# Loading two weight blocks ahead of the transposes, spreading by pairs of offsets, and a new order of steps

## The chip, the cores and the metric

The kernel runs on one core of a Trainium2 chip. The metric is the device time in microseconds of one execution, as the median of several runs. The profile is one further execution, recorded instruction by instruction; its span runs from the first instruction to the last. Engines: PE is TensorE's matmul side and PEld its weight loads, DVE is VectorE, ACT is ScalarE, POOL is GpSimd, SP is SyncE, which here only issues DMA.

## What is computed

Two independent halves whose results are put side by side. Half A is attention with 32 heads of 20 channels over 2048 positions, in which each position looks at 8 earlier ones, 2 apart. Half B is a state-space layer: a kernel K of length 2048 for each of 640 channels from 192 complex exponentials, and its causal convolution with u.

```python
# A: x [1, 2048, 640], wqkv [640, 1920], wo [640, 640]
q, k, v = split(x @ wqkv)                       # 32 heads of 20
idx = pos[:, None] - 2 * arange(8)[None, :]     # masked where negative
attn = softmax(einsum("bhsd,bhswd->bhsw", q, k[idx]) * 20**-0.5)
a = einsum("bhsw,bhswd->bhsd", attn, v[idx]).reshape(1, 2048, 640) @ wo

# B: u [1, 2048, 640]; A, B, C complex [640, 192]; dt = exp(log_dt)
P = exp((dt * A)[:, :, None] * bf16(arange(2048)))
K = einsum("dn,dnl,dn->dl", C, P, dt * B).real
y = irfft(rfft(u, 4096) * rfft(K, 4096))[:2048] + u * Dskip
out = concatenate([a, y], axis=-1)              # [1, 2048, 1280]
```

The positions of B are taken in bf16, so above 256 many positions share one rounded value. K is therefore computed at few distinct values only and then spread to all positions by matrices of zeros and ones.

## The kernel before, in words

**Steps and their order.** The program is written as 1772 small steps, each an instruction or a short run of them, collected by `st(...)` under the name of a stage. Nothing runs when a step is collected. `run` (L191) then calls the steps in the order of the list of numbers `ORDER` (L20), and each engine works through its own instructions in exactly that order. A step that waits holds all later ones of its engine. So `ORDER` is the schedule, written out by hand or by a program that is not part of the kernel.

**Start.** Six parameter arrays of half B are loaded ("nat", L297). A tiny store on SyncE (L326) waits for two of them and holds back what follows in SyncE's queue: four DMA transposes that load x with channels on the partitions ("xT", L330), 512 positions each. GpSimd looks at one element of the same parameters ("peek", L336), then loads the weights of q and k (L342), looks at one element of xT (L347), and then loads u (L353) and the weights of v (L342). Two small stores (L332, L333) put zeros ahead of k and v. TensorE turns the parameters (L381 to L390) and DVE and ACT make from them exponentials, sines and cosines (L448 to L466); those of chunks 1 to 4 go through memory ("Gdram", L469).

**Half A.** For k, q and v, 5 channel tiles and 4 position blocks, five 128x512 matmuls make a projection (L587), ACT casts it (L590), and SyncE stores it (L592). Later, for 4 blocks of positions, DVE forms products (L748), TensorE sums them (L753), ACT takes the exponential (L756), the weights are normalised (L773 to L789), DVE multiplies v by them (L804), TensorE sums (L809), ACT casts (L812), and a last matmul with wo (L823), a cast (L826) and a store end it.

**Half B.** The 640 channels go in 5 chunks. For each chunk DVE builds two tables, X (L188 to L190) and Y (L188 to L190, L544), TensorE contracts them (L561, 512 small matmuls a chunk) and the result is stored ("Kdram", L568). It comes back as K2 (L662), and stage "g" spreads it (L668 to L681): four steps of matmuls, one for each quarter of the 32 channels (`tq`); in each, for 8 offsets `j`, one or two 0/1 matrices and 4 groups of partitions, a matmul with 64 (or 32) columns (L677); after each step ACT copies the bank out (L681). `f1` (L633) transforms u and K (L641, L646), which takes one channel at a time, stage "x" does the second transform and the product (L696 to L703), "back" the inverse (L717, L723), and the last matmuls with HB (L886) go together with u times Dskip into the output.

Of the kernel before, what the change touches and what calls it, by code (L numbers as in the profile page):

```python
# [20 lines left out]
1 3 8 9 24 0 4 5 7 6 26 338 30 31 32 33 35 34 36 37 51 329 39 74 327 17 38 73 80 77 40 41 42 43 44 79 78 76 53 55 45 48 334 50 56 46 61 102 16 81 71  # L21
336 335 321 333 52 54 47 58 49 57 62 60 59 128 63 64 75 25 72 103 332 326 104 129 130 108 131 123 67 105 109 21 18 19 132 66 110 111 106 133 724 118
124 125 92 65 119 27 29 126 121 337 120 93 107 94 95 68 70 127 87 122 112 89 88 20 28 82 83 84 96 294 293 97 296 295 113 297 90 91 298 85 98 99 100 86
726 727 114 115 730 116 300 134 299 301 302 192 117 731 135 303 136 150 137 101 194 725 69 728 23 22 193 304 138 305 168 306 151 195 153 152 186 169
729 732 187 170 171 308 847 307 843 188 189 310 309 317 312 311 142 145 766 190 146 762 763 143 144 147 174 198 760 761 767 339 196 172 139 314 313 2
141 148 149 199 154 315 844 848 316 764 765 706 331 330 325 322 328 324 197 707 323 811 845 318 841 319 173 320 340 175 176 180 342 341 191 155 177
200 178 710 343 344 210 201 346 345 202 708 812 712 768 709 711 846 849 182 181 204 713 805 806 836 348 347 211 837 213 212 183 214 184 850 842 856
349 809 810 156 205 179 807 808 834 206 162 207 835 832 833 714 203 350 838 839 157 215 185 351 352 721 719 158 159 717 163 722 164 165 245 247 851
857 353 852 854 813 140 160 371 370 354 208 209 161 246 239 275 718 720 715 840 413 716 408 355 403 356 357 166 375 374 376 377 378 379 380 381 383
382 384 385 386 387 388 389 410 219 778 784 358 167 359 11 372 373 391 390 398 393 392 240 218 407 414 409 723 779 416 855 853 417 785 222 782 226 224  # L30
241 242 257 248 360 780 783 395 394 249 781 276 361 746 362 363 742 277 278 397 396 402 364 243 223 399 786 279 744 743 401 747 217 400 365 366 367
420 423 424 426 419 745 425 427 428 220 411 415 406 405 251 412 250 404 748 749 750 735 221 736 259 737 739 455 738 258 260 740 430 429 791 792 281
261 431 432 733 368 734 252 454 253 418 789 790 787 254 255 434 433 458 459 788 793 741 435 794 461 460 269 462 463 244 436 465 464 795 437 421 422
216 280 751 752 13 466 467 225 753 754 757 758 771 772 282 271 283 755 756 775 262 227 256 10 469 468 284 270 287 776 769 770 456 470 471 482 229 285
457 472 473 272 288 273 474 228 230 475 233 476 477 231 438 478 479 369 773 774 759 439 1343 802 289 777 440 798 290 291 480 441 442 803 481 263 496
799 234 814 483 815 800 443 274 286 1342 796 235 801 236 797 237 264 265 485 266 444 484 267 1344 292 820 445 804 821 823 446 827 825 824 1345 447 232
1346 448 488 1347 268 495 490 487 493 491 1348 238 541 1350 828 497 449 1349 1352 498 829 1351 450 826 1353 830 831 492 451 504 1355 503 501 1356 1357
500 489 1354 494 486 499 1358 1359 816 502 1360 818 817 1361 1363 507 508 510 509 512 511 506 539 819 822 1362 538 1364 505 1365 1366 1367 1368 858
514 513 515 516 542 517 518 519 864 543 1369 545 544 452 1374 12 520 546 547 522 865 873 1370 863 875 867 549 548 862 1402 1371 521 550 551 866 1373
881 882 876 874 879 880 868 871 872 869 583 859 877 878 870 883 884 887 1387 888 889 890 885 540 886 901 895 1372 553 860 552 902 1375 555 554 1377  # L40
557 556 566 559 558 893 1376 894 896 903 905 904 1378 1401 906 897 898 899 900 891 892 523 14 1403 1379 1388 923 924 580 1389 561 919 917 920 921 453
918 922 926 560 943 944 1404 925 1405 941 939 940 937 907 942 938 945 563 911 562 912 1390 1391 908 909 910 564 565 946 524 525 15 1406 927 913 1381
1407 526 914 1380 916 1382 928 579 571 576 584 1392 527 933 934 960 929 931 1384 1383 932 930 978 567 936 1393 528 1385 1429 568 969 970 1395 1394
1396 1398 1428 935 569 973 974 975 961 962 861 965 1430 1397 529 530 531 532 574 966 581 1432 1431 1399 1400 1441 1386 585 1433 572 575 582 573 533
1486 578 976 1442 1434 963 977 1435 1436 534 1437 535 588 587 586 570 1438 1439 536 1443 1444 577 971 1440 1466 1445 1446 1447 1449 983 972 592 591
594 964 623 967 590 968 593 984 915 595 596 1413 985 1448 1450 1414 995 622 997 1451 1452 1453 986 597 598 1454 996 599 600 1455 601 602 626 627 628
629 603 631 630 998 1001 979 980 999 604 589 1415 1002 632 633 1416 1000 981 982 989 987 990 988 1417 1408 991 992 993 1410 994 605 1017 1037 1487
1411 1409 1018 635 634 625 1456 1457 1038 636 637 1056 1412 956 958 957 947 949 948 953 954 955 1033 1034 1035 1013 1490 1014 1420 1039 1019 1036 1040
1015 950 1016 1020 1021 661 1022 638 951 606 1514 1513 1517 1042 1418 1419 1009 639 537 1488 1423 664 641 1041 1007 1005 640 657 1006 952 607 1010
1003 608 666 1421 609 610 1425 1023 1424 624 1489 1491 1008 1004 1024 1465 1469 1467 611 1011 642 643 1029 1030 650 1027 1472 1492 645 644 1028 1012  # L50
646 647 1057 1063 1025 1468 1470 1473 1026 1058 1074 658 1474 663 655 1064 612 649 648 667 1476 656 662 613 1422 1471 614 1426 1059 1073 1060 1067
1068 1061 1069 1070 1079 615 1475 616 1477 1062 1479 1478 1071 1072 1480 1458 1459 1460 1065 1066 1462 1461 1481 617 1463 1464 1515 651 1483 1081 1032
1031 1482 618 619 1080 1093 1094 1091 1092 1516 1518 674 1484 652 653 659 1519 1427 620 672 1082 676 675 1521 1485 665 1097 1098 1077 1075 1076 1078
677 678 1520 1523 1089 668 671 679 680 654 681 682 684 683 685 660 669 670 687 673 959 1085 1090 1086 1505 1095 1096 1503 688 686 689 1504 1522 1083
1087 1084 1524 1088 1525 1052 1099 1053 1100 1054 1506 1498 1049 1050 1051 1043 1044 1101 1045 1102 1500 1105 1103 1046 1104 1106 1108 1129 1131 1048
621 1047 690 1130 1132 1507 1495 1135 1133 1136 1134 1119 1125 1107 1170 1120 1126 1551 1499 1138 1137 1123 1124 1109 691 1152 692 1121 1111 693 1110
1122 1112 1526 1527 1528 1115 1116 1113 1163 1572 1114 1153 1529 1159 1164 1530 1501 1531 1161 694 1154 1532 1155 1533 1160 1167 1169 1534 1535 695
1162 1156 1550 1536 1537 696 1117 1496 1168 1599 1502 1538 1539 1571 1165 1493 1157 1158 1166 1540 1541 1171 1172 1179 1180 1542 1494 1552 1177 1173
1175 1176 1174 1178 1510 1508 1553 1511 1509 1128 1554 1555 1556 1575 1573 1189 1185 1183 1190 1186 1598 1600 1118 697 1574 1181 1187 1191 1184 1192
1576 1544 1543 1545 1547 698 1193 1188 1194 1182 1546 1195 699 700 1548 1565 1564 1566 1197 1199 1577 1567 1127 1568 701 1569 702 1207 1497 1196 1558  # L60
1557 1561 1559 1055 1200 1198 1208 1602 703 1601 1549 1560 1604 1603 704 1562 1570 1209 1605 1563 1210 1512 1142 1606 1143 1607 1148 1201 1144 1149
1150 1608 1588 1211 1202 1205 1609 1212 1139 1206 1611 1145 1613 1204 1203 1610 1140 1589 1215 1590 1213 1580 1141 1214 1146 1147 1591 1216 1221 1231
1225 1222 1219 1578 1229 1612 1232 1226 1220 1227 1230 1228 1234 1217 1218 1247 1248 1249 1254 1255 1628 1252 1253 1250 1251 1581 1650 1256 1257 1579
1258 1262 1260 1263 1649 1683 1614 1688 705 1689 1691 1692 1693 1259 1265 1264 1272 1615 1261 1273 1223 1616 1268 1270 1269 1271 1286 1266 1267 1288
1287 1278 1289 1279 1617 1618 1619 1620 1621 1629 1151 1592 1224 1282 1595 1596 1283 1284 1280 1622 1281 1285 1593 1274 1275 1690 1698 1276 1277 1699
1582 1233 1594 1583 1730 1733 1734 1735 1290 1736 1291 1737 1738 1294 1295 1731 1732 1623 1624 1625 1626 1687 1302 1303 1694 1627 1306 1304 1292 1307
# [147 lines left out]
def kernel(  # L214
# [126 lines left out]
    def ld_w(i):  # L341
        PQ.dma_start(out=wqkv[i]()[:], in_=wsrc[:, :, D * i:D * i + D])  # L342

    for i in (1, 0):
        st(lambda i=i: ld_w(i))
# [591 lines left out]
```

The softmax here doesn't subtract the row's maximum and nothing guards it: scores larger than these inputs give would overflow.

## Time and profile before

| | before |
|---|---|
| time, median of 3 (lowest to highest) | 377.85 us (376.5 to 384.24) |
| span of the profiled run | 378.9 us |
| instructions | 14759 |
| granted TensorE clock, mean | 0.891 |
| DMA | 72.54 MB, mean 191 GB/s |
| ACT table loads | 13 of 1283 ns |

In the page, the busy time of an engine is the sum of its instructions with overlaps counted once. A group line reads: line, engine, operation, output from inputs, shape, count, then busy time and mean time of one, then the idle time of the engine just before these instructions and what ended it. In the list of waits, the engine and line that waited stand first, then what ended the wait, the total, the number of times and the longest. "Issue" means that the engine waited for nothing that the profile shows.

### The profile page before, as it was taken

To read this page: it belongs to the slowest core of one execution; us is meant where nothing else is said; L and a number is where in the kernel's file an instruction comes from. 1 tells how busy PE (TensorE), PEld (TensorE's weight loads), DVE (VectorE), ACT (ScalarE), POOL (GpSimd) and SP (SyncE) were. 2 spreads that over 40 slices of the span, in tenths; PEclk is the share of its full clock that TensorE was granted. 3 is DMA by queue.
4 is the path that set the end of the run, shared out by engine and by line. 5 is a ranking of instruction groups with operands and counts; after the bars stand their busy time and mean duration, and the time that the engine had idled before them with its cause. 6 is when DMAs were issued, how large, how long until landed. Compare 5 with 4: busy or idle time off the path is not lost.

```text
span 378.9 us, 14759 instructions
## 1 busy us (share of the span) xinstructions
PE 295.5 (78%) x6431; PEld 195.2 (52%) x6431; DVE 311.5 (82%) x467; ACT 274.1 (72%) x604; POOL 64.9 (17%) x123
## 2 busy tenths in 40 slices
PE   1704765999999992658889789679997799798872
PEld 1601222455545550636655557556775558576751
DVE  1891799798999999996999986999967956769770
ACT  2980998899999972369557667577867559898651
POOL 3021012110000003512402022005001211001181
PEclk9955896999999998589668889988999969999997
DMA  7999658656567648955908573243626979869777
GB/s 175 143 162 291 153 162 295 207 194 234 184 215 245 200 147 253 270 129 169 216 13 210 144 210 89 74 143 114 180 79 188 301 255 293 260 201 331 203 154 174
DMA packets 59696, 72.54 MB, mean 191 GB/s; under 512 B 24344, under 2 KB 49544, under 8 KB 58864
## 3 DMA queue, kind: packets, MB, share of 16 engines
q1 hardware_dynamic: 53760, 54.91, 50.8%
q0 software_dynamic: 5296, 15.96, 16.6%
q8 instruction: 50, 0.82, 0.9%
q10 hardware_dynamic: 576, 0.74, 0.6%
q14 instruction: 14, 0.11, 0.1%
HBM read 43.98 MB, written 24.98 MB: 182 GB/s over the span
## 4 chain that ended last, share of the span: by engine, by line
PE 25%; ACT 13%; DVE 11%; issue 8%; DMA 2%; ACTq 0%; SPq 0%; DVEq 0%
PE ps_f L641 5%; ACT S L700 5%; PE ps_op L823 5%; PE ps_k L561 4%; DVE p L804 3%; PE ps_ia L717 3%; ACT Z L723 3%; ACT A L646 3%; PE ps_f L696 2%; PE ps_l L753 2%; PE ps_o L809 1%; DVE Yf L703 1%; PE ps_s L677 1%; DVE krtmp L188 1%; DVE prod L748 1%
## 5 line engine op out<-in xcount | busy, mean ns | idle before, releaser
L587 PE MATMUL ps_p<-xT,w 128*128 128x512 bf16 x300 | 75.6, 402 | 27.2 <-DMA xT<-in_A_x_dram 17.6
L561 PE MATMUL ps_k<-Ytab,Xtab 128*20 128x33 bf16 (+1 forms) x2560 | 53.2, 245 | 14.5 <-DVE Ytab L544 9.0
L587 PEld LDWEIGHTS <-w 128*128 128x128 bf16 x300 | 28.9, 102 | 66.8 <-issue 36.9
L646 ACT CAST A<-ps_f 128x512 bf16<-128x512 f32 x80 | 44.1, 620 | 25.2 <-PE ps_f L641 14.1
L561 PEld LDWEIGHTS <-Xtab 128*20 128x20 bf16 (+1 forms) x2560 | 45.5, 126 | 27.5 <-issue 24.1
L748 DVE TENSOR_TENSOR prod<-qb,kb 128x2048 bf16<-128x2048 bf16 x40 | 47.1, 1219 | 7.1 <-PE ps_l L753 7.0
L804 DVE TENSOR_TENSOR p<-vb,attn 128x2048 bf16<-128x2048 bf16 x40 | 47.6, 1218 | 6.2 <-PE ps_o L809 6.1
L700 ACT CAST S<-ps_f 128x512 bf16<-128x512 f32 x80 | 43.0, 613 | 8.4 <-PE ps_f L696 4.5
L590 ACT CAST st<-ps_p 128x512 bf16<-128x512 f32 x60 | 33.5, 580 | 16.9 <-PE ps_p L587 16.8
L797 POOL DMA_DIRECT2D vb<-vd x40 | 22.0, 556 | 96.3 <-DVE p L804 92.0
L703 DVE TENSOR_TENSOR Yf<-S 128x1024 bf16<-128x1024 bf16 x40 | 26.4, 686 | 7.9 <-ACT S L700 6.1
L696 PE MATMUL ps_f<-A,cT 128*64 128x128 bf16 x640 | 28.8, 228 | 1.9 <-ACT A L646 0.9
L823 PE MATMUL ps_op<-wo,oT 128*128 128x320 bf16 x160 | 29.2, 327 | 0.6 <-ACT ob L826 0.6
L696 PEld LDWEIGHTS <-cT 128*64 128x64 bf16 x640 | 21.0, 113 | 11.3 <-issue 9.4
L522 ACT ACTIVATE Stab<-ta 128x192 bf16<-128x192 f32 x80 | 24.4, 367 | 0.1
L809 PE MATMUL ps_o<-p,cG 128*32 128x512 bf16 x160 | 17.4, 445 | 8.5 <-DVE p L804 7.7
L723 ACT CAST Z<-ps_ia 128x512 bf16<-128x512 f32 x40 | 21.5, 607 | 3.3 <-PE ps_ia L717 3.2
L717 PE MATMUL ps_ia<-cEA,Yf 64*128 64x128 bf16 x640 | 21.8, 221 | 1.6 <-ACT ysb L891 0.7
L641 PE MATMUL ps_f<-cBD,U 128*64 128x128 bf16 x320 | 21.6, 293 | 0.0
L717 PEld LDWEIGHTS <-Yf 64*128 64x128 bf16 x640 | 19.0, 96 | 4.8 <-issue 3.5
L641 PEld LDWEIGHTS <-U 128*64 128x64 bf16 x320 | 19.4, 205 | 3.1 <-issue 2.2
L188 DVE TENSOR_TENSOR krtmp<-Xtab,Xg 128x1536 bf16<-128x1536 bf16 (+2 forms) x30 | 20.5, 682 | 0.3 <-DMA Xtab<-Gdram 0.3
(105 smaller groups left out, 515.8 us busy)
## 6 DMA issues: line engine op xcount, KB each, us to landing
vb<-vd SPq DMA_DIRECT2D x40, 128.5 KB, 5.3
vb<-vd POOLq DMA_DIRECT2D x40, 128.5 KB, 4.2
Gdram<-cs SPq DMA_DIRECT2D x22, 192.0 KB, 2.9
HB<-k_HB SPq DMA_DIRECT2D x8, 512.0 KB
Zdram<-Z SPq DMA_DIRECT2D x3, 1024.0 KB
zq<-Zdram SPq DMA_DIRECT2D x12, 256.0 KB, 5.1
kb<-kd SPq DMA_DIRECT2D x4, 657.5 KB
us<-in_B_u_dram POOLq DMA_DIRECT2D x2, 1280.0 KB, 7.5
```

Source lines behind the costliest of these rows:

```text
L561: MM(ps()[32 * g:32 * g + 20, i, :], lhsT=X[c]()[rows, part % 2, :, col + t0 + i], rhs=Y[c]()[rows, :, part % 2, col + t0 + i], start=(par ...
L587: MM(ps()[:], lhsT=w()[:, kt, 128 * ct:128 * ct + 128], rhs=xT()[:, kt, 512 * sc:512 * sc + 512], start=(kt == 0), stop=(kt == 4))
L590: st(lambda so=so, sc=sc, ps=ps: ACTE.copy(out=so()[:, sc], in_=ps()[:]))
L641: MM(ps()[64 * r:64 * r + 64, jj], lhsT=src(16 * dd + 4 * jq + jj), rhs=BD1()[:, r, :], start=(jj == 0), stop=True, skip_group_check=True, ...
L646: st(lambda o=o, ps=ps: ACTE.copy(out=A1[c]()[:, :, sig, o:o + 16].rearrange("p k (j g) -> p k j g", g=4), in_=ps()[:].rearrange("p j (k g ...
L696: MM(ps()[64 * dd:64 * dd + 64, kk, r], lhsT=T()[:, k, r, :], rhs=A1[c]()[:, k, :, 64 * dd:64 * dd + 64], start=(kk == 0 and r == 0), stop ...
L700: st(lambda h=h, ps=ps, Sp=Sp: ACTE.copy(out=Sp()[:, :, :, :, 2 * h:2 * h + 2, :].rearrange("p r s j k g -> p (r s) j k g"), in_=ps()[:].r ...
L717: MM(ps[dd]()[:, jj].rearrange("p l r -> p (l r)"), lhsT=Yf[c]()[d, q, 4 * jq + jj, :], rhs=EA()[d, q, :], start=(jj == 0 and q == 0), sto ...
L723: st(lambda o=o, ps=ps, dd=dd: ACTE.copy(out=zc()[:, :, :, o:o + 4].rearrange("p l r j -> p (l r) j"), in_=ps[dd]()[:].rearrange("p j l r ...
L748: st(lambda pr=pr, ct=ct, u2=u2: V.tensor_tensor(out=pr()[:], in0=q()[:, ct].unsqueeze(1).to_broadcast([128, 4, PB]), in1=windows(k()[:, c ...
L804: st(lambda p2=p2, u2=u2: V.tensor_tensor(out=p2()[:], in0=v()[:, :, 2 * u2:2 * u2 + PB], in1=attn[b]()[:, u2].unsqueeze(1).to_broadcast([ ...
L823: MM(ps()[:], lhsT=oT[b]()[:, t, 128 * x:128 * x + 128], rhs=wo_sb()[:, t, 320 * eh:320 * eh + 320], start=(t == 0), stop=(t == 4))
```

## The change

It has four parts. First, the weights of q and k are loaded by GpSimd right after the parameters, and SyncE's tiny stores, which hold back the transposes, now wait for these weights instead of a parameter array; the weights of v and u follow, as before, behind a look at xT. The aim is that weight loads and transposes no longer share the DMA engines. Second, the spread goes by pairs of offsets: a step takes two offsets `j` and all 32 channels, so a matmul has 256 (or 128) columns in place of 64 (or 32), there are a quarter as many, and ACT's copy of a step fills two offsets of every channel instead of all offsets of eight channels. Third, all steps come in a new order; in SyncE's queue the constants Gs and RB and the two halo stores now stand ahead of the transposes, two of which are ahead of the first store to Gdram and two behind it. Fourth, the identity and the peeked element lie in another pool of SBUF.

```diff
 ORDER = """
-1 3 8 9 24 0 4 5 7 6 26 338 30 31 32 33 35 34 36 37 51 329 39 74 327 17 38 73 80 77 40 41 42 43 44 79 78 76 53 55 45 48 334 50 56 46 61 102 16 81 71
...
+16 3 8 9 0 4 7 5 1 17 6 31 32 33 19 18 21 10 12 34 20 26 27 25 24 28 36 35 38 37 53 39 75 40 41 42 322 74 78 333 326 77 55 81 43 44 57 49 73 72 45 46
...
-    ident = const("cst", "ident", np.eye(128), [128, 128])
+    ident = const("prep", "ident", np.eye(128), [128, 128])
...
-    tiny = dpool.tile([1, 2, 2], bf16, name="tiny")
+    peek = tl("prep", [1, 2, 2], bf16, "peek")
+    st.stage("igb")
+    st(lambda: PQ.tensor_copy(out=peek()[:], in_=nat[4][0]()[0:1, :, 0, 0:2]))
+    st.stage("iw")
+    wsrc = A_wqkv.rearrange("(kt k) c -> k kt c", k=128)
+    wqkv = [tl("xw", [128, 5, D], bf16, f"w{i}") for i in range(3)]
...
+    for i in (1, 0):
+        st(lambda i=i: ld_w(i))
+    tiny = dpool.tile([2, 2], bf16, name="tiny")
     st.stage("iga")
-    st(lambda: SP.dma_start(out=tiny[:], in_=nat[4][0]()[0:1, :, 0, 0:2]))
+    for i in (1, 0):
+        st(lambda i=i: SP.dma_start(out=tiny[i:i + 1], in_=wqkv[i]()[0:1, 4, D - 2:D]))
     st.stage("ix")
     xT = tl("xw", [128, 5, S], bf16, "xT")
...
-    peek = tl("cst", [1, 2, 2], bf16, "peek")
-    st.stage("igb")
-    st(lambda: PQ.tensor_copy(out=peek()[:], in_=nat[4][0]()[0:1, :, 0, 0:2]))
-    st.stage("iw")
...
-    for i in (1, 0):
-        st(lambda i=i: ld_w(i))
...
-        for tq in range(4):
-            ts = slice(8 * tq, 8 * tq + 8)
-            ps = bank([128, 8, 8, 8], "ps_s", "b")
-
-            def go(ts=ts, ps=ps):
-                for j in range(8):
-                    for n_, (w, par) in enumerate(plan[j]):
+        for jp in range(4):
+            ps = bank([128, 2, 8, 32], "ps_s", "b")
+
+            def go(jp=jp, ps=ps):
+                for jj in range(2):
+                    for n_, (w, par) in enumerate(plan[2 * jp + jj]):
                         sel = slice(0, 8) if par is None else slice(par, 8, 2)
                         for g in range(4):
-                            MM(ps()[32 * g:32 * g + 32, j, sel], lhsT=SEL()[:, w, :], rhs=K2()[:, g, sel, ts], start=(j == 0 and n_ == 0), stop=True,
+                            MM(ps()[32 * g:32 * g + 32, jj, sel], lhsT=SEL()[:, w, :], rhs=K2()[:, g, sel], start=(jj == 0 and n_ == 0), stop=True,
                                tile_position=(0, 32 * g), skip_group_check=True)
 
             st(go)
-            st(lambda ts=ts, ps=ps: ACTE.copy(out=K()[:, ts].rearrange("p t (b j) -> p t b j", j=8), in_=ps()[:].rearrange("p j b t -> p t b j")))
+            st(lambda jp=jp, ps=ps: ACTE.copy(out=K()[:].rearrange("p t (b j) -> p t b j", j=8)[:, :, :, 2 * jp:2 * jp + 2], in_=ps()[:].rearrange("p j b t -> p t b j")))
         f1(c, lambda t: K()[:, t], 1)
```

## The prediction

> **What bounds the kernel now.** I read the page's first part and the table by stages first, since no engine fills the span.
>
> ```profile
> PE 295.5 (78%) x6431; PEld 195.2 (52%) x6431; DVE 311.5 (82%) x467; ACT 274.1 (72%) x604; POOL 64.9 (17%) x123
> ```
>
> ```profile
> 0.00:20.00 20.00, 8.89 (x120) 7.59 (x120) 10.27 (x23) 12.09 (x34) 3.04 (x10) 0.99 1.02 152
> 20.00:40.00 20.00, 6.64 (x15) 1.94 (x15) 10.40 (x36) 8.73 (x29) 3.71 (x4) 0.50 1.11 239
> 40.00:145.00 105.00, 92.94 (x1361) 46.70 (x1361) 98.97 (x172) 97.47 (x208) 8.60 (x15) 0.97 0.63 204
> ...
> 300.00:379.00 79.00, 63.29 (x1412) 47.02 (x1408) 50.76 (x57) 54.42 (x116) 15.94 (x28) 0.93 0.81 236
> ```
>
> Columns: stretch, length, busy PE, PEld, DVE, ACT, POOL, then granted clock, DMA share and GB/s. VectorE carries the most work (311.5 us) and is idle for 67 us of the 378.9. From 40 to 145 us DVE, ACT and PE are all nearly full, so little is to be had there. The idle time lies at the start (10 us before the first data, 10 more between 20 and 40 us) and after 300 us (28 us, of which some 9 are the last projection and its store). Next, the list of waits for the two places that the change touches:
>
> ```profile
> PE ps_p L587 <- DMA xT<-in_A_x_dram: 17.6, 3, 12.8
> ACT st L590 <- PE ps_p L587: 16.8, 8, 10.3
> DVE ph L462 <- ACT Xg L464: 10.7, 2, 9.6
> PE ps_s L677 <- issue: 6.2, 4, 3.4
> ```
>
> The first three are one event, as the timeline of ACT and DVE shows:
>
> ```profile
> 27.23 0.44 ACT L465 ACTIVATE Ytab<-mc,quarter 128x192 bf16<-128x192 f32 x1
> 37.98 0.58 ACT L590 CAST st<-ps_p 128x512 bf16<-128x512 f32 x1 [10.31 <-PE ps_p L587]
> ```
> ```profile
> 28.99 0.55 DVE L188 TENSOR_TENSOR krtmp<-Xtab,Xg 128x768 bf16<-128x768 bf16 x1
> 39.11 0.36 DVE L462 TENSOR_SCALAR ph<-wi 128x384 int32<-128x384 int32 x1 [9.57 <-ACT Xg L464]
> ```
>
> A cast of the first projection stands in ACT's queue at a point that ACT reaches at 27.67 us. Its matmuls wait for the transposed x, so ACT stands for 10.31 us, and DVE for 9.57 us behind it. Why x is late shows in the DMA's windows of 2 us (last column GB/s) and in SyncE's timeline:
>
> ```profile
> 16.00:18.00 2.00, 0.57 (x5) 0.34 (x4) 2.00 (x6) 2.00 (x8) 0.00 (x0) 1.00 1.24 40
> 18.00:20.00 2.00, 0.00 (x0) 0.00 (x0) 1.97 (x4) 1.99 (x5) 0.00 (x0) 0.91 1.30 62
> ...
> 32.00:34.00 2.00, 0.00 (x0) 0.00 (x0) 0.00 (x0) 0.00 (x0) 0.00 (x0) 0.50 0.90 333
> ```
> ```profile
> 5.15 33.86 SPq L330 DMA_TRANSPOSE xT<-in_A_x_dram  x4
> ```
>
> While transposes and weight loads are mixed, the DMA moves 40 to 62 GB/s; with the v and u loads alone it moves 333. The four transposes hold SyncE's queue for 33.86 us, though the shortest takes 3.28 us.
>
> **What the Trainium skill says.** "TensorE: Matmul & The Clock Gate", section "Architectural detail: the array is 16× 32×32, not 1× 128×128": ACT and DVE are strict FIFO. The trace agrees: both stand 10 us behind one blocked cast. The same page, "What's actually happening": the PE clock is gated to half by default and released by sustained activity; the trace grants 0.50 between 20 and 40 us, where PE is idle, and 1.00 in the dense stretches. "DMA: Bandwidth & Descriptors", section "Issuing engines are not separate DMA queues": transfers from SyncE and GpSimd interleave on the same 16 engines. That fits the mixed stretch, though the page doesn't promise so deep a fall as 40 GB/s.
>
> **The change part by part.**
>
> *Weights of q and k ahead of the transposes.* Two small stores on SyncE now wait until q and k have landed; the four transposes stand behind them. The two loads are 1.6 MB; at the 277 to 294 GB/s that the DMA gives between 2 and 6 us they take 5.7 us from about 6 us, so they land at 12 to 13. Behind the waiting stores stand only two constants, the two halo stores (0.7 us each to issue) and the transposes: the first two run from about 15.5 to 22.5 us at 3.3 us each. Then the peek on GpSimd (2.2 us) releases u and v, 2.1 MB, some 7 us at 300 GB/s, to about 31. The other two transposes stand behind the store of Gt, which DVE finishes after 16.0 us of its work, at about 25 us; they mix with u and v until 31 and land at about 36. Before, the last landed at about 41.
>
> *Where the first cast now stands.* I priced both instruction lists with the mean durations of the rows of before. Ahead of the first cast ACT had 21.0 us of work; it has 33.6 now. Before, ACT was at 27.67 us with 21.0 done, an offset of 6.7; so it meets the cast at about 40 us, 4 us after the last x. The stall of 10.31 us on ACT and of 9.57 on DVE should vanish. Bounds: 0 (x late again, or PE binding) to 11 us (all, and a little of 8 later short stalls at the same line). PE is the reason for not taking 11: by 40 us it has done 15 us of work in both kernels. But from there it was fed by ACT, which is now 10 us ahead. I take -9.
>
> *Spread.* L677 had 720 matmuls (9 matrices, 4 groups, 4 quarters, 5 chunks); now there are 180 with 256 or 128 columns. The columns streamed are the same. The nearest row is the one of attention sums, also on 32-column tiles:
>
> ```profile
> L753 PE MATMUL ps_l<-prod,cGs 128*32 128x512 bf16 x160 | 17.7, 444 | 2.0 <-DVE prod L748 1.9
> L677 PE MATMUL ps_s<-K,cSEL 128*32 128x64 bf16 (+1 forms) x720 | 9.5, 194 | 6.7 <-issue 6.2 <-ACT A L646 0.3
> ```
>
> 17.7/160 is 111 ns per 512 columns, so 55 for 256 and 28 for 128: per chunk 28 x 55 + 8 x 28 = 1.8 us, in all 8.8, the upper bound. The lower one uses the price in "TensorE: Matmul & The Clock Gate", section "Back-to-back issue gap": 262 cycles for 256 columns (109 ns at its 2.4 GHz) and four tiles at once, an estimate of 8 x 109 ns = 0.9 us per chunk, 4.4 in all. So busy time hardly falls: 9.5 to 8.8. What falls is the 6.2 us in which PE waited for nothing visible inside these runs; the page's word is "issue", and it stands in the chain of waits with 3.36 us at 162.3, 1.04 at 287.2 and 1.53 at 326.3. With 1080 fewer PE instructions here (720 pairs to 180), I expect most of it to go. Of 5.9 us on the chain I take -4; bounds 0 and -6.
> Against it: a transform of K needs all offsets, so its first matmul now waits for four ACT copies (0.63 us each) where one was enough. That is 3 x 0.63 = 1.9 us a chunk, 9.5 in five, if nothing else stands between; PE has u transforms, projections and table matmuls to fill with. I take +2; bounds 0 and 9.5.
>
> *Order of steps.* ACT table loads fall from 13 to 11 in the new list, 2 x 1.28 us; ACT binds only up to 145 us, so -1. The larger matter is the end. When DVE stands at 261 us of its work (some 300 us in the trace), the list of before leaves PE 67 us and ACT 56; the new list leaves 52 and 42. The last table matmuls (L561) stand at 246 us of DVE work instead of 264, and the last inverse at 306 instead of 311. So in the stretch of 79 us, where PE is busy 63, 15 us of PE and ACT work go to an earlier one. That earlier stretch, 145 to 300 us, had PE at 124 of 155 us and can take it: 139 of 155 is below the 94% that PE reaches from 60 to 145. Of 15 us I take two thirds, -10, since chains of PE, ACT and DVE are not all filled. Bounds: +10 (a new stall like the one of 10.31 us, elsewhere) and -15. Two constants and a scratch tile in another pool move nothing: SBUF space alone.
>
> Sum: 377.85 - 9 - 4 + 2 - 1 - 10 = 355.85, say 356.
>
> **The rivals.**
> (1) Only the start is gained; new waits cost what the order and the spread bring: 377.85 - 10 = 368. For it: 28 us of DVE idle time after 300 us come from chains that no order removes altogether. Against it: PE and ACT have 15 us less to do there.
> (2) DVE becomes the bound nearly throughout: 311.5 + 10 at the start + 9 at the end + 15 in between = 346. For it: the balanced sums. Against it: even between 145 and 230 us, with PE at 62 of 85, DVE is idle 5 us.
> (3) No gain or slower: PE has done the same 15 us of work by 40 us and needs 280 more with the 58 us of idle it had after that, so the start brings nothing: 40 + 280 + 58 = 378; with the waits for four copies, 9.5 us, 387. For it: PE's list behind the first casts is as long as before. Against it: much of PE's idle time from 40 to 60 us (6.9 us) was waiting for ACT.
>
> **How the numbers follow.** Forecast 356: 0.50. Rival (1), 368: 0.22. Rival (2), 346: 0.13. Rival (3), 378 to 387: 0.15. Predicted is 356. The range goes from 344, a little below (2), to 374: it takes in (1) and nearly all of the +10 bound on the order (355.85 + 20 = 376), and leaves (3) out. A 2% gain is under 370.3, a 2% loss over 385.4: faster has all of the forecast and of (2), and about two thirds of (1), 0.77; same takes the rest of (1) and half of (3), 0.14; slower 0.09.
>
> **What would show it.** Right: ACT's wait for the first cast gone or under 3 us; the clock still 0.50 at 20 to 35 us; transposes of about 3.3 us for the first two; the group of the spread at 180 matmuls, 7 to 9 us busy and under 2 us of "issue"; DVE's idle time after its 261st us of work down from 28 us to below 20. Wrong: a new idle time of 5 us or more on ACT or DVE in front of one instruction; the waits of transforms for the copies of K over 5 us in all; PE at 95% from 40 us on, with DVE waiting for it.

## The result, and the profile after

The changed kernel takes 354.62 us (median of 4 runs, 351.94 to 360.72). The kernel before, run beside it, took 381.05 us (376.5 to 387.65). The ratio is 0.938, with a 95% interval of 0.921 to 0.955. Here and below times are medians of all runs, while ratios are taken over the fast runs alone (within 1.5% of the kernel's fastest; here 353.7 against 377.2 us), so by the ratio 23 us are gone and by the medians 26. The forecast was 356 us.

The engines do about the same work as before. What has shrunk is idle time, as the first part of the page of the changed kernel shows:

```profile
PE 287.2 (82%) x5870; PEld 190.2 (54%) x5891; DVE 309.8 (89%) x467; ACT 272.0 (78%) x602; POOL 64.3 (18%) x123
```

DVE has 1.7 us less to do, but it is idle for 40 us of the 349.9 us span instead of 67. Where those 27 us were shows in the table by stages of the changed kernel (stretch, length, busy PE, PEld, DVE, ACT, POOL, then granted clock, DMA share and GB/s):

```profile
0.00:20.00 20.00, 10.90 (x130) 8.15 (x131) 11.12 (x28) 13.21 (x36) 2.84 (x9) 1.00 0.67 194
20.00:40.00 20.00, 6.78 (x17) 1.99 (x18) 20.00 (x51) 19.84 (x54) 4.33 (x7) 0.63 0.99 254
40.00:145.00 105.00, 95.57 (x1474) 51.14 (x1494) 97.78 (x165) 89.62 (x192) 14.59 (x31) 0.94 0.72 230
145.00:275.00 130.00, 112.84 (x3189) 85.57 (x3184) 121.19 (x163) 99.94 (x219) 25.64 (x47) 0.95 0.57 161
275.00:350.00 75.00, 61.11 (x1071) 43.34 (x1070) 59.74 (x64) 49.36 (x105) 16.92 (x30) 0.93 0.88 246
```

Between 20 and 40 us DVE and ACT are now full, where they had 10.40 and 8.73. In the last 75 us DVE is busy for 59.7; in the last 79 of the kernel before it was 50.8. Between 40 and 145 us nothing is gained; DVE has 1 us less there. The list of waits of the changed kernel for the same places:

```profile
PE ps_p L588 <- DMA xT<-in_A_x_dram: 14.6, 3, 10.4
DVE uc L602 <- DMA Udram<-uc: 5.1, 2, 4.1
DVE p L804 <- PE ps_o L809: 3.9, 4, 3.0
```

PE still waits for x, 14.6 us after 17.6. ACT and DVE no longer stand behind it: of the 16.8 us of ACT for the projections 1.4 are left, and the 10.7 us of DVE at L462 are gone. DVE has one new stall, of 4.1 us, at 69.3 us (L602). SyncE's and ACT's timelines show why ACT no longer waits:

```profile
15.23 7.06 SPq L343 DMA_TRANSPOSE xT<-in_A_x_dram  x2
...
25.13 11.54 SPq L343 DMA_TRANSPOSE xT<-in_A_x_dram  x2
```
```profile
38.75 1.56 ACT L591 CAST st<-ps_p 128x512 bf16<-128x512 f32 x3
```

The third transpose, whose x the first cast needs, lands at 36.4 us (35.5 before), and the last at 39.3 (41.0). PE has the bank full at 38.71 us, ACT comes to the cast at 38.75 and finds three banks ready: no bracket with an idle time follows. So x isn't earlier for this cast than it was; ACT comes later. Last, the groups of the spread, of the transforms of K behind it and of the copies between them:

```profile
L677 PE MATMUL ps_s<-K,cSEL 128*32 128x256 bf16 (+1 forms) x180 | 8.1, 297 | 0.1
...
L642 PE MATMUL ps_f<-cBD,K 128*64 128x128 bf16 x320 | 12.8, 222 | 4.3 <-ACT K L681 4.1
L681 ACT CAST K<-ps_s 128x512 bf16<-128x512 f32 x20 | 12.2, 750 | 3.4 <-PE ps_s L677 3.4
```

The spread's own busy time fell from 9.5 to 8.1 us, and the 6.2 us of "issue" ahead of it are gone (0.1 of idle time is left). The transforms of K in the kernel before, for comparison:

```profile
L641 PE MATMUL ps_f<-cBD,K 128*64 128x128 bf16 x320 | 15.3, 242 | 4.4 <-ACT K L681 2.7 <-issue 1.7
```

A table worked out from the traces is used below: the time at which DVE has done so many us of its work (durations added up, overlaps once; the end of the instruction that passes the mark). DVE's own list is hardly changed in length, so a difference between two columns is a lead. The columns are single profiled runs; those of before and after lie 29.0 us apart (378.9 and 349.9 us).

| DVE's work done, us | before | cast_later | order_only | after |
|---|---|---|---|---|
| 20 | 39.5 | 29.4 | 29.3 | 28.9 |
| 100 | 125.3 | 114.4 | 116.9 | 116.0 |
| 160 | 188.5 | 178.2 | 182.5 | 179.2 |
| 240 | 273.9 | 263.2 | 272.4 | 262.3 |
| 260 | 299.8 | 291.3 | 298.3 | 286.0 |
| 300 | 356.1 | 348.7 | 344.1 | 328.1 |
| DVE's last end | 367.5 | 360.1 | 354.5 | 338.2 |

The changed kernel wins 10.6 us in the first 20 us of DVE's work, holds 9 to 12 up to 240, and wins a further 17.7 from there to the end.

### The profile page after: what moved, and what is told of

Read it like the earlier page. It is cut to its first block, busy times and chain, and to the rows that moved or that the text cites. A ratio compares the mean times of both kernels' runs of the same rounds, so it can differ in the third digit from the quotient of the medians.

```text
span 349.9 us, 13661 instructions
## 1 busy us (share of the span) xinstructions
PE 287.2 (82%) x5870; PEld 190.2 (54%) x5891; DVE 309.8 (89%) x467; ACT 272.0 (78%) x602; POOL 64.3 (18%) x123
## 5 line engine op out<-in xcount | busy, mean ns | idle before, releaser
L588 PE MATMUL ps_p<-xT,w 128*128 128x512 bf16 x280 | 72.1, 395 | 18.6 <-DMA xT<-in_A_x_dram 14.6
L804 DVE TENSOR_TENSOR p<-vb,attn 128x2048 bf16<-128x2048 bf16 x40 | 47.3, 1218 | 6.0 <-PE ps_o L809 3.9
L647 ACT CAST A<-ps_f 128x512 bf16<-128x512 f32 x80 | 43.3, 664 | 7.7 <-PE ps_f L642 7.0
L797 POOL DMA_DIRECT2D vb<-vd x40 | 22.5, 568 | 56.8 <-DVE p L804 44.8
L696 PE MATMUL ps_f<-A,cT 128*64 128x128 bf16 x640 | 28.1, 224 | 3.7 <-ACT A L647 1.9
L823 PE MATMUL ps_op<-wo,oT 128*128 128x320 bf16 x160 | 27.3, 317 | 0.7 <-ACT oT L812 0.7
L703 DVE TENSOR_TENSOR Yf<-S 128x1024 bf16<-128x1024 bf16 x40 | 25.8, 682 | 0.0
L523 ACT ACTIVATE Stab<-ta 128x192 bf16<-128x192 f32 x80 | 25.1, 370 | 0.0
L812 ACT CAST oT<-ps_o 128x512 bf16<-128x512 f32 x20 | 13.0, 656 | 11.5 <-PE ps_o L809 11.4
L826 ACT CAST ob<-ps_op 128x320 bf16<-128x320 f32 x32 | 14.1, 462 | 10.1 <-PE ps_op L823 8.0
L753 PE MATMUL ps_l<-prod,cGs 128*32 128x512 bf16 x160 | 16.9, 406 | 5.4 <-DVE prod L748 4.8
L823 PEld LDWEIGHTS <-oT 128*128 128x128 bf16 x160 | 14.9, 103 | 11.1 <-issue 3.3
```

Source lines behind the costliest of these rows:

```text
L523: st(lambda k=k: ACTE.activation(out=Stab[c]()[:, k - 1], in_=ta()[:, CW * c:CW * c + CW], func=ACT.Exp, scale=float(-16 * k)))
L588: MM(ps()[:], lhsT=w()[:, kt, 128 * ct:128 * ct + 128], rhs=xT()[:, kt, 512 * sc:512 * sc + 512], start=(kt == 0), stop=(kt == 4))
L647: st(lambda o=o, ps=ps: ACTE.copy(out=A1[c]()[:, :, sig, o:o + 16].rearrange("p k (j g) -> p k j g", g=4), in_=ps()[:].rearrange("p j (k g ...
L696: MM(ps()[64 * dd:64 * dd + 64, kk, r], lhsT=T()[:, k, r, :], rhs=A1[c]()[:, k, :, 64 * dd:64 * dd + 64], start=(kk == 0 and r == 0), stop ...
L703: st(lambda b=b, i=i, Sp=Sp: V.tensor_tensor(out=Yf[c]()[:, 2 * i:2 * i + 2, :, 32 * b:32 * b + 32], in0=Sp()[:, :, 1].rearrange("p r j k ...
L797: (SP if q else PQ).dma_start(out=v()[32 * g:32 * g + 32], in_=vd[:, 4 * dg:4 * dg + 4, PB * b + 4 * g:PB * b + 4 * g + PB + 2])
```

## The experiments

The theory was the prediction's sum: the start gives 9 us (loads and place of the cast), the spread 2 net, the order 11. The runs take the three parts apart. They were made in three groups, each with its own runs of the kernel before beside it (381.08 us for the first four rows, 384.66 for the next four, 382.24 for the last three); ratios are to these, with their 95% intervals.

| run | what it is | us, median | ratio |
|---|---|---|---|
| order_only | new order alone | 365.15 | 0.967 (0.959 to 0.975) |
| loads_only | new loads alone | 380.23 | 1.004 (1.001 to 1.008) |
| after_old_loads | changed kernel, old loads | 352.99 | 0.934 (0.929 to 0.940) |
| after_old_spread | changed kernel, old spread | 366.42 | 0.969 (0.961 to 0.978) |
| spread_only | new spread alone | 378.34 | 0.980 (0.973 to 0.987) |
| after_split4 | changed kernel, 720 spread matmuls | 366.19 | 0.953 (0.947 to 0.958) |
| after_split2 | changed kernel, 360 spread matmuls | 355.08 | 0.923 (0.919 to 0.928) |
| after_less_dve | changed kernel, five DVE operations fewer | 350.59 | 0.909 (0.904 to 0.915) |
| after_again | changed kernel | 355.21 | 0.934 (0.924 to 0.943) |
| cast_later | kernel before, first casts later | 372.53 | 0.976 (0.967 to 0.985) |
| cast_later_spread | the same and the new spread | 365.83 | 0.960 (0.951 to 0.970) |

**The loads alone.** The kernel before takes over the new loads and the stores that wait for them. In ORDER (whose numbers shift a little, since a step is added) the two stores, now 20 and 21, stand directly ahead of the first transpose, and the old store is dropped:

```diff
-    tiny = dpool.tile([1, 2, 2], bf16, name="tiny")
-    st.stage("iga")
-    st(lambda: SP.dma_start(out=tiny[:], in_=nat[4][0]()[0:1, :, 0, 0:2]))
...
+    for i in (1, 0):
+        st(lambda i=i: ld_w(i))
+    tiny = dpool.tile([2, 2], bf16, name="tiny")
+    st.stage("iga")
+    for i in (1, 0):
+        st(lambda i=i: SP.dma_start(out=tiny[i:i + 1], in_=wqkv[i]()[0:1, 4, D - 2:D]))
```

> The weights of q and k ahead of the transposes, in the old order and with the old spread. My theory: the four transposes are through by about 30 us instead of 41, the stall of ACT at the first cast falls from 10.3 to 3 us or less, and -7 us are kept to the end, ratio 0.98. Rival: the stall goes but comes back later, since PE has the same work before it; ratio 0.995 or more.

Measured: 1.004, the time of the rival, but not for its reason, since the stall is still there. SyncE's and ACT's timelines of this run:

```profile
12.95 22.05 SPq L343 DMA_TRANSPOSE xT<-in_A_x_dram  x4
```
```profile
37.38 0.59 ACT L591 CAST st<-ps_p 128x512 bf16<-128x512 f32 x1 [9.57 <-PE ps_p L588]
```

The transposes are through SyncE's queue by 35.0 us instead of 39.0, so the idea works as far as it goes. But GpSimd's look at x now succeeds at 20.1 us (26.4 before), and u and v, which it releases at 20.6 and 21.3 us (28.5 and 29.2 before), meet the remaining transposes. PE's second group of matmuls, the one that the first cast needs, starts at 35.05 us (35.65 before), and ACT, which reaches the cast at 27.7 to 27.8 us in either kernel, still waits 9.57 us for it.

**The order alone.** The kernel before, with the changed kernel's ORDER translated to its own numbers (the steps of the spread and of the loads in the corresponding places); no other line changes. The start of the list:

```diff
-1 3 8 9 24 0 4 5 7 6 26 338 30 31 32 33 35 34 36 37 51 329 39 74 327 17 38 73 80 77 40 41 42 43 44 79 78 76 53 55 45 48 334 50 56 46 61 102 16 81 71
...
+16 3 8 9 0 4 7 5 1 24 6 30 31 32 26 25 17 10 12 33 22 23 21 20 27 35 34 37 36 52 38 74 39 40 41 321 73 77 332 325 76 54 80 42 43 56 48 72 71 44 45 46
...
```

> The new order of steps alone, with the old loads and the old spread. My theory: the first cast now stands at 33.6 us of ACT's work, so most of the 10 us stall at the start is gone even though the last x still lands at about 41 us (3 to 4 us of it are left), and the end is shorter by some 10 us: about -17 us, ratio to before 0.955. Rival A, the start is cured by the loads alone: only the end is gained, -10, ratio 0.973, with a stall of 8 us or more at the first cast. Rival B, the order brings nothing by itself: ratio 0.99 or more.

Measured: 0.967, between the theory (0.955) and the first rival (0.973), of which the theory's lies just outside the interval and the rival's inside. The rival's stall at the first cast isn't there: in the table above this run has a lead of 10.2 us at 20 us of work, only 1.5 at 260, and 13.0 at the end. So the order gives at both ends and takes in between.

**The changed kernel with the old loads.** The new loads go back to the old ones, and SyncE's old store stands where the two new ones stood:

```diff
-    for i in (1, 0):
-        st(lambda i=i: SP.dma_start(out=tiny[i:i + 1], in_=wqkv[i]()[0:1, 4, D - 2:D]))
+    st(lambda: SP.dma_start(out=tiny[:], in_=nat[4][0]()[0:1, :, 0, 0:2]))
```

> The changed kernel with the old loads (transposes beside the weight loads). My theory: the last x lands at about 41 us instead of 36, ACT stands 3 to 5 us at the first cast, and the time rises by as much over the changed kernel: ratio to before 0.948 where the changed kernel has 0.938. Rival: the place of the cast hides all of it; within 1 us of the changed kernel. Other rival: the loads were worth the whole 9 us; ratio 0.96 or more.

Measured: 0.934, the same as the changed kernel (0.934 to 0.938). SyncE's and PE's timelines of this run:

```profile
7.45 11.57 SPq L330 DMA_TRANSPOSE xT<-in_A_x_dram  x2
...
25.01 8.44 SPq L330 DMA_TRANSPOSE xT<-in_A_x_dram  x2
```
```profile
33.11 2.31 PE L587 MATMUL ps_p<-xT,w 128*128 128x512 bf16 x5 [10.53 <-DMA xT<-in_A_x_dram]
```

The x for the first cast is there at 33.11 us, 3.3 us sooner than with the new loads, where the theory had it later. The first of the transposes beside the weights is slow (7.96 us), though less so than the first two in the kernel before (8.91 and 12.31); the last two meet u and v only until 28.8 us (32.4 with the new loads). What parts them is the order: two of the transposes stand behind the store of Gt. In both kernels ACT comes to the cast at 38.4 to 38.8 us, after x, and with the old loads the bank has been full for 3 us by then (35.42 us). So in either order the new loads are worth nothing that can be measured.

**The place of the first cast.** What is left for the start is the place of the cast. In the kernel before, the steps of the projections from the first cast on (727) are held back until 57 other steps have gone by, and are then let in one after every two others, until the two lists agree again some 50 steps later. The matmuls of these projections move with their casts; the lists of DVE, GpSimd and SyncE stay as they were:

```diff
-726 727 114 115 730 116 300 134 299 301 302 192 117 731 135 303 136 150 137 101 194 725 69 728 23 22 193 304 138 305 168 306 151 195 153 152 186 169
+726 114 115 116 300 134 299 301 302 192 117 135 303 136 150 137 101 194 69 23 22 193 304 138 305 168 306 151 195 153 152 186 169 187 170 171 308 847
+307 843 188 189 310 309 317 312 311 142 145 190 146 143 144 147 174 198 339 196 727 172 139 730 314 313 731 2 141 725 148 149 728 199 154 729 315 844
...
```

> The kernel before with one thing of the new order: the first casts of the projections stand behind some 10 us more of ACT's work. Theory (the stall of 10.31 us belongs to the place of the cast): ACT waits under 3 us for the first cast, DVE has done 20 us of work at about 30 us instead of 39.5, and 7 us or more of that reach the end: 0.98 or lower. Rival (the lead is used up by waits later, since the rest of the order is as before): the stall is gone as well, but the time is 0.99 to 1.00.

Measured: 0.976, the theory. ACT's timeline of this run:

```profile
39.52 0.56 ACT L590 CAST st<-ps_p 128x512 bf16<-128x512 f32 x1
```

The 10.31 us are gone, with the old loads and x no earlier than before (PE's matmuls for this cast start at 35.66 us, 35.65 before). In the table DVE's lead is 10.1 us at 20 us of work and still 7.4 at the end. Some 9 us by the ratio (6 to 12 by its interval) are thus shown to come from where the first casts stand in the order.

**The spread, taken out and put in.** First the changed kernel with the old spread, the other way round from the diff of the change: 720 matmuls of 64 or 32 columns in the same places of the same order.

```diff
-        for jp in range(4):
-            ps = bank([128, 2, 8, 32], "ps_s", "b")
...
+        for tq in range(4):
+            ts = slice(8 * tq, 8 * tq + 8)
+            ps = bank([128, 8, 8, 8], "ps_s", "b")
```

> The changed kernel with the old spread (720 matmuls of 64 columns by quarters of the channels). My theory: idle PE time with nothing visible comes back at the spread (4 to 7 us against 0.1), the wait for four copies goes, and the time rises by 2 us over the changed kernel (bounds 0 and 6), ratio to before 0.943. Rival A, the waits of PE at the spread are all on the path: +6 us, ratio 0.954. Rival B, the four copies cost more than the matmuls saved: the kernel becomes faster than the changed one, ratio under 0.934.

Measured: 0.969, or 366.42 us, 11 to 12 more than the changed kernel and twice what the prediction allowed at most. (order_only is this kernel with the old loads, and has 365.15 us.) The groups and the waits of this run show where they are:

```profile
L678 PE MATMUL ps_s<-K,cSEL 128*32 128x64 bf16 (+1 forms) x720 | 9.8, 203 | 6.0 <-issue 5.1 <-ACT A L647 0.9
```
```profile
DVE p L805 <- PE ps_o L810: 15.9, 11, 3.5
ACT A L647 <- PE ps_f L642: 11.2, 10, 2.7
ACT K L682 <- PE ps_s L678: 9.2, 6, 3.2
```

The matmuls themselves and the idle time just ahead of them account for 1.7 + 5.9 = 7.6 us of PE. But DVE, in the attention part (L804 in the changed kernel, L805 here), now waits 15.9 us for PE's sums instead of 3.9. DVE's idle time up to its last instruction is 44.0 us in this run and 28.4 in the profiled run of the changed kernel. The difference, 15.6 us, is what came at two lines: ahead of this one idle time went from 6.0 to 15.9 us, and ahead of Yf (L703, here L704), which waits for ACT's casts of S, from 0.0 to 5.7. (The two profiled runs are 15.9 us apart, more than the medians.) DVE is delayed far from the spread, by PE work that stands behind it.

The granted clock doesn't explain most of it. It is lower here (0.897 in the profiled run, 0.926 in the changed kernel's), but runs with 0.906 to 0.908 took 354.55 and 356.71 us with the new spread, and 363.88 with the old one.

Then the kernel before with the new spread alone. 17 steps of transforms move behind the last of the four copies, which they now need:

```diff
-                            MM(ps()[32 * g:32 * g + 32, j, sel], lhsT=SEL()[:, w, :], rhs=K2()[:, g, sel, ts], start=(j == 0 and n_ == 0), stop=True,
+                            MM(ps()[32 * g:32 * g + 32, jj, sel], lhsT=SEL()[:, w, :], rhs=K2()[:, g, sel], start=(jj == 0 and n_ == 0), stop=True,
```

> The new spread in the old order with the old loads; 17 steps that would read K before its four copies are moved behind the last copy. Theory, PE's supply of instructions: 1080 fewer instructions on PE save about 12 us here too, ratio to before 0.97. Rival, the new spread needs the new order, since its four copies hold up what follows: within 1% of before.

Measured: 0.980, some 7.7 us (5 to 10 by the interval), between the two expectations. In the order of before the spread is worth less. There is also less to win at the place that cost most in the new order, in the kernel before and then with the new spread:

```profile
DVE p L804 <- PE ps_o L809: 6.1, 3, 2.9
```
```profile
DVE p L803 <- PE ps_o L808: 2.9, 2, 2.0
```

**Number of instructions or arrangement.** The new spread differs from the old one in three ways: fewer matmuls, another layout of the bank, other copies. In the next two kernels each matmul of the changed kernel is cut along its columns into four or two, with banks, copies and order as they are:

```diff
-                        for g in range(4):
-                            MM(ps()[32 * g:32 * g + 32, jj, sel], lhsT=SEL()[:, w, :], rhs=K2()[:, g, sel], start=(jj == 0 and n_ == 0), stop=True,
-                               tile_position=(0, 32 * g), skip_group_check=True)
+                        for h in range(4):
+                            hs = slice(8 * h, 8 * h + 8)
+                            for g in range(4):
+                                MM(ps()[32 * g:32 * g + 32, jj, sel, hs], lhsT=SEL()[:, w, :], rhs=K2()[:, g, sel, hs], start=(jj == 0 and n_ == 0 and h == 0), stop=True,
+                                   tile_position=(0, 32 * g), skip_group_check=True)
```

> The changed kernel with each matmul of the spread cut into four of a quarter of the columns: same banks, same copies, same place in the order, but 720 pairs of weight load and matmul again in place of 180. Theory, supply of instructions: as slow as with the old spread, 366 us, ratio 0.969, with idle PE time with nothing visible at the spread. Rival, it is the arrangement by pairs and its copies that helped: as fast as the changed kernel, 0.938.

> The same with each matmul cut into two: 360 pairs, a third of the added instructions. Theory: a third of the loss, +4 us over the changed kernel, ratio 0.948. If PE catches up on fetching between the runs of small matmuls, less than that: 0.938 to 0.943.

Measured on one chip: 366.19 us with four, 355.08 with two. Four pieces cost as much as the old spread, so the number of PE instructions is the cause, and layout and copies are not. The groups and the waits of the kernel cut in four, then those of the kernel cut in two:

```profile
L679 PE MATMUL ps_s<-K,cSEL 128*32 128x64 bf16 (+1 forms) x720 | 9.7, 200 | 6.8 <-issue 6.0 <-ACT A L647 0.8
```
```profile
DVE p L806 <- PE ps_o L811: 15.2, 10, 5.3
```
```profile
L679 PE MATMUL ps_s<-K,cSEL 128*32 128x128 bf16 (+1 forms) x360 | 8.1, 235 | 0.0
```
```profile
DVE p L806 <- PE ps_o L811: 3.3, 6, 1.7
```

Two pieces cost nothing that can be told (355.08 beside 354.62 and 355.21 on other chips), so the cost isn't proportional: it sets in between 360 and 720 matmuls in these places.

**Why PE stands in "issue".** The page lists a DMA queue that carries instructions, in the kernel before and in the changed one:

```profile
q8 instruction: 50, 0.82, 0.9%
```
```profile
q8 instruction: 46, 0.75, 0.9%
```

Both are packets of 16 KB, and 12862 PE instructions over 50, or 11782 over 46, is some 256 a packet. (Cut in two, 47 packets; cut in four, 50.) The times of the packets, set beside the count of instructions that PE has started, show that this queue feeds PE and that PE runs out. In the kernel before PE stops five times at exactly 449 instructions plus 256 for each packet that has landed, and goes on 1.4 to 1.6 us after the next one has. The 3.36 us of "issue" from 162.34 us are one of these stops: PE had started 3521 instructions, which is 449 + 12 x 256, the next packet landed at 164.29 us, and PE went on at 165.70. The five stops are 10.2 us of idle time. With the old spread in the new order there are ten with 18.1 us, at the spread and at other lines; with four pieces eight with 15.9, with two pieces four with 6.7, in the changed kernel two with 4.5. (In the last three traces 21 matmul records are missing, and the count is 21 lower.) So the old spread has 13.6 us of such stops more than the new one, and four pieces 9.2 more than two, close to the differences in time.

In all thirteen traces no packet starts less than 3.35 us after the one before: 256 in 3.35 us is 76 per us. In bursts PE starts more, up to 161 in one us in the kernel before and 216 with the old spread in the new order; over ten us at most 64 to 80. The small matmuls of the old spread, on four tiles, go 72 in 0.83 us at 160.39 us in the kernel before, with as many weight loads. That is 173 per us, over twice what arrives for long; after 132 of the 144 pairs of that chunk came the stop of 3.36 us. The Trainium skill, "Runtime: NRT & Kernel Launch", section "Instruction fetch mechanics", describes refills in blocks of 16 KiB, 256 instructions, and calls the cost of crossing a block mostly hidden. The block agrees with the packets here; "mostly hidden" doesn't hold for runs of small matmuls on four tiles. What keeps the packets 3.35 us apart, no run here tells.

**Is DVE the bound now?** The changed kernel without the five operations of DVE that negate Stab (L548); one of the two parts of Y's lower half keeps the wrong sign, so this part of the computation is left out:

```diff
-        st(lambda: V.tensor_scalar(out=Stab[c]()[:], in0=Stab[c]()[:], scalar1=-1.0, scalar2=None, op0=A.mult))
+        st(lambda: None)
```

> The changed kernel without the five VectorE instructions that negate Stab (0.96 us each, 4.8 us in all, in the steps of the Y tables); this leaves out a sign in the imaginary half of Y. If VectorE bounds the changed kernel up to its last instruction, as its 310 us of work in 335 suggest, the time falls by 4 to 5 us, ratio 0.926. If chains through PE and ACT bind instead, by 1 us or less, ratio 0.936.

Measured: 350.59 us, 4.5 less than the kernel cut in two on the same chip, and 4.0 to 4.6 less than the changed kernel elsewhere. The five had 4.8 us in their group, and DVE's busy time in the page, with overlaps counted once, is 3.9 us less (305.9 instead of 309.8). What DVE is spared comes off the end nearly one to one, within the 3 us or so that the intervals leave open.

**The parts put together.** The changed kernel again, and the kernel before with the later casts and the new spread (the two edits above):

> The changed kernel once more, beside the two kernels below on one chip: 0.935 of the kernel before (352 to 358 us).

> The same with the new spread too, in the old order otherwise. If the later cast and the spread add: 0.96. If the spread is worth 12 us once DVE is ahead, as in the new order: 0.95. If the later cast brings nothing to the end: 0.98, as with the spread alone. What is then missing to 0.935 belongs to the rest of the new order.

Measured on one chip: 0.934 and 0.960. By the ratios, the later cast brings 9 us, the new spread on top of it 6, and the rest of the order (with the new loads) 10 more; by the medians 9.7, 6.7 and 10.6. The intervals of 0.976 and 0.960 just overlap, so the middle number is the least certain. One more reservation belongs to it. In the profiled run of cast_later_spread, the slowest of its six (370.87 us), PE's and DVE's timelines show x late and a new stall:

```profile
41.86 4.35 PE L587 MATMUL ps_p<-xT,w 128*128 128x512 bf16 x10 [11.72 <-DMA xT<-in_A_x_dram]
```
```profile
61.03 0.36 DVE L462 TENSOR_SCALAR ph<-wi 128x384 int32<-128x384 int32 x1 [10.65 <-ACT cs L464]
```

The transposes took till 43.6 us in SyncE's queue; the first store of exponentials to memory (L469) stood behind them and behind a projection's store, till 50.7 us; and ACT, which waits for such a store of cs at 55 us (4.1 us), holds up DVE. That run had lost the whole lead of the cast by 100 us of DVE's work (125.7 us). In the profiled run of spread_only, also its slowest, the x for the first cast came as late (42.18 us). In the other three runs with four transposes in a row that have a trace it came at 35.05 to 35.66 us, and in the eight with the transposes split around the store of Gt at 32.0 to 37.8. So with four in a row the place of the cast alone may not be safe; whether the other runs of these two kernels had such a stall isn't known.

## Why the prediction was right, point by point

**The sum was right, one term twice its bound and one reason idle.** Forecast were 356 us (344 to 374), measured 354.62. In part that is luck. Taken one after another by the ratios, the place of the cast gives 9 us (cast_later), the rest of the order 3.5 (order_only) and the new spread 11 to 12, where the forecast had 9, 11 and 2: what the order fell short of, the spread brought.

*Weights of q and k ahead of the transposes.* The first times were right: q and k landed at 11.1 and 13.3 us (12 to 13 predicted), the first two transposes went from 15.23 to 22.29 us at 3.5 us each (15.5 to 22.5 at 3.3), the x for the first cast landed at 36.4 us. The last x, predicted for 36, landed at 39.3. I used these times as the reason why x is there for the cast, and the loads are not needed for that: with the old loads this x came at 33.1 us in the new order, and alone the new loads gave 1.004. The reading behind it was too narrow as well: the 40 and 62 GB/s of the mixed stretch are its two lowest windows, and the other windows of 2 us from 10 to 24 us moved 134 to 243. What the step overlooked is that the look at x releases u and v as soon as the first quarter is there, so an earlier first quarter only brings the next collision forward.

*Where the first cast now stands.* The -9 were right. ACT met the cast at 38.75 us (40 predicted), the wait is gone, and the place alone gave 9 us (0.976). The reasoning by offsets, 33.6 us of ACT work ahead instead of 21.0, holds. The 4 us to spare were not there: PE had the bank full at 38.71 us, because its five matmuls took 2.3 us after x at 36.4. That the stall is gone altogether was close, and it is the new loads that used up the 3 us which the old ones leave.

*Spread.* This is the step that failed in size: -4, bounds 0 and -6, against 7.7 us in the old order and 11 to 12 in the new one. The row was read rightly (busy 8.1 us after 8.8 predicted, "issue" 0.1), but I took the "issue" idle time in front of the spread's own matmuls for the whole cost. The same shortage also delays the PE work behind them, and DVE, which is close to being the bound, pays for it at other lines (15.9 us of idle time ahead of L804 with the old spread, 6.0 with the new; 5.7 and 0.0 ahead of Yf). A wider bound could have been read from the trace of before: 540 pairs fewer are 1080 instructions, 4.2 packets of 256, and at the 3.54 us that lie at least between two packets that is 15 us. What was measured lies below it and above mine.

*Waits for four copies.* +2, bounds 0 and 9.5. The wait of the transforms for the copies went from 2.7 to 4.1 us, +1.4.

*Order of steps.* -10 and -1 for the tables. After the part that belongs to the cast, the order brought 3.5 us with the old spread (0.976 to 0.967, within the intervals) and 10 with the new one (0.960 to 0.934). DVE's idle time after its 260th us of work is 14 us (27.6 before; below 20 was predicted): 63.9 us of span with 49.8 of work. The loss in between (the lead of order_only falls from 10 to 1.5 us by the 260th us) wasn't foreseen. Work moved out of the end must be done there, and PE ran out of instructions six times between 146 and 263 us in that run (10.4 us in all); no run tells the two apart. With the new spread the lead is still 13.8 us at the 260th us. The two table loads fewer (11 after 13) were seen, but no run measures them alone.

*The signs.* Those of the first cast, the spread and DVE's end came as said. The clock, which was to be 0.50 from 20 to 35 us, was 0.67 there. A new idle time of 5 us on DVE was to be a sign of being wrong: the one at L602 has 4.1 us in the trace above and 4.1 to 5.3 in all eight traces of the new order.

**The rivals.** (1), only the start is gained, 368 us: cast_later is that case, and its 0.976 is 369 of 377.85 us, so the size was right, but the spread and the order do bring more. (2), DVE bound nearly throughout, 346 us: 9 us too low, but with a point, since a microsecond less on DVE is nearly a microsecond less in the end, and DVE's idle time is down to 40 us (34 in the rival's sum). (3), PE's list is too long for the start to matter: refuted by cast_later, whose lead of 10.1 us came to the end with 7.4.

## What to carry to other kernels

A cast at a wrong place in an in-order queue can cost as much as a slow transfer, here some 9 us; count the work ahead of it on its engine and compare with the time when its input lands, before the transfer is made faster. Idle time called "issue" in front of many small matmuls can be a shortage of instructions: count them against the packets that bring them, and look for the cost at whatever engine waits for the work behind. Here, halving 720 pairs brought the whole gain and quartering them no more.

## What the runs showed that was not expected

- PE's instructions arrive at no more than some 76 per us for long (256 in 3.35 us at the least; at most 80 started per us over any ten us), while it starts up to 216 in one us. When it has started all that arrived it stands until 1.0 to 1.6 us after the next packet has landed. 720 small pairs cost 11 to 12 us more than 180, and 360 cost nothing more.
- Loads that are separated from transposes of x at their head can meet them at their tail. With transposes done 4 us earlier, and u and v released 8 us earlier, PE's second group of matmuls on x began at 35.05 us instead of 35.65, and the time was 1.004 of before.
- With the old loads in the new order, two transposes beside the weight loads took 11.57 us in SyncE's queue and the other two 8.44, in all less than the 33.86 us of all four in a row in the kernel before.
